# One ring of 28 rows, 12 kept rows and three spectral input buffers in a fused forward and backward pass

## The chip, the cores and the metric

The kernel runs on one core of a Trainium2 chip. The metric is the device time of one execution in microseconds (us), and lower is better. The engines are named as in the profile: PE (TensorE, matrix products), DVE (VectorE), ACT (ScalarE), POOL (GpSimd) and SP (SyncE), from whose queue every DMA of this kernel is issued. A row below is a block of 128 tokens by 512 features in bf16; there are R = 16 rows.

## The reference

With q, k, v of 2048 tokens by D = 512 features, and F = 1376 hidden features, the output is the sum of three terms:

```
xn  = layernorm(q)
kv  = (causal convolution of k with shift_k, 4 taps) * v
y   = irfft(rfft(kv padded to 4096) * rfft(ssm_k padded)) [first 2048] + kv * ssm_D
out = q + xn * y + ((xn @ w_gate) * (xn @ w_up)) @ w_down
```

Given grad_out, the kernel returns out and the gradients of q, k, v, shift_k, ssm_k, ssm_D, w_gate, w_up and w_down: ten outputs in all. The backward pass needs the same long convolution with the roles of its factors exchanged, and the products of the gated unit with respect to inputs and weights.

## The kernel before

**Stages.** The kernel is one program of about 8200 instructions with five stages that overlap.

1. *Start.* q and grad_out are loaded. DVE normalises the rows into `xn`, and PE transposes them into `XT`. A few products on constants run first.
2. *The gated unit, in six steps over F* (`glu_gen`, `mlp_rows(j, r)`). The widths of the steps are 256, 96 and four times 256 columns. For each pair of rows PE computes `pd` (grad_out by w_down) and `pg` (xn by w_gate and w_up). ACT and DVE copy them to `gu`, and DVE multiplies them into three tensors per row, called the hd rows: h, and the two factors of the gradient. They go into a ring in SBUF. `dw_gen(j)` reads 16 ring rows of a step to form the weight gradients. `hd_store(j, r)` writes them to the DRAM buffer HD. Step 5, the last one, and the last KEEP rows of step 4 are not written: `turn_gen` has PE transpose them, eight 128x128 blocks at a time, and ACT copy them back over the ring.
3. *Stage A* (`a_gen`). DVE forms the short convolution and the products kv and dy. PE applies the first factor of a Fourier transform built by hand, ACT copies the result into a buffer `ax`, and a DMA stores it to the DRAM buffer AX.
4. *The spectral stage* (`s_gen`), eight rounds i. `s_load(2i)` and `s_load(2i+1)` read AX into the buffers `sa`. `s_B(i)` applies the second factor on PE, `s_pw` multiplies the spectra on DVE, `s_Bi(i)` transforms back, and its result is stored to the DRAM buffer CX.
5. *The last stage, F,* eight chunks n of two rows. `c_load(n)` reads CX, and `last_dft(n)` applies the last factor on PE. `c_dkv`, `c_y`, `c_o5`, `c_dsk` and `dk_pair` form the gradients of v, k, ssm_k and shift_k and the term xn*y, mostly on DVE. `hd_load(n)` is a DMA transpose that reads the hd rows of two rows from HD into `hdP[n % 2]`. `y_o(n, rr)` multiplies the hd blocks by w_down for out, and `y_x(n, rr)` multiplies them by w_gate and w_up for the gradient of q. Small loads (`dkv_load`, `y_load`, `k_load`) fetch rows of v, KS (the short convolution, stored by stage A), x and k.

**What sets the order.** No queue or heuristic decides at run time. Every compute instruction and every DMA is recorded first, and `emit` replays the records in an order written out in the string `PLAN`, which also assigns each PSUM slot. The order on each engine is therefore fixed. An instruction waits when the data, the buffer or the PSUM slot is not ready, and all instructions behind it on its engine or queue wait with it. Since the recorder issues every instruction, all of them carry its line, L172, in the profile.

**Memory.** SBUF is divided by hand into regions: `rX` (xn and grad_out), the ring from 34 KB, `rT` (the transposed inputs, later the weights `wy`), `rW` (weights of the steps, later `hdP`) and `RA` (the buffers of stage A, then of the spectral stage, then of stage F, one after the other in the same bytes). The ring has 24 rows of 1536 bytes; step 0 has a 24 KB buffer of its own at `RH0`, inside `RA`. The lines that the change touches are these:

```
KEEP = 8
RING = 24
ax = [ra.tile(f"ax{i}", [128, 2, 3, D]) for i in range(2)]
ksA = ra.tile("ksA", [128, 2, D])
sp["a"] = [m.tile(f"sa{i}", [128, 2, 3, D]) for i in range(4)]
def hd_span(n):
    return (0, 1152) if 2 * n < R - KEEP else (128, 1024)
```

`hd_span` gives the rows of HD that `hd_load(n)` moves: with KEEP = 8 all 1152 rows for n = 0 to 3, and 896 for n = 4 to 7.

Of the kernel before, what the change touches and what calls it, by code (L numbers as in the profile page):

```python
# [10 lines left out]
BF = mybir.dt.bfloat16  # L11
# [17 lines left out]
KEEP = 8  # L29
RING = 24  # L30
EPS = 1e-5
PLAN = "c-k#j1GFx^4o%Xa=i0Vy+qP}nwr$(CZQHhO^L^+3Z%wCZGRf{v)~snJG#~(k0S94$AU=eH@W2oOB0?mH3<3%UQJ?^%fT$1+QbJlt1s;MR1f+(75E4Q`8i)?*pbDgi43H6GKqiO@RUr#xhOCeu3PDMT1=*ko6oyie9ZEwEhz&&{CzOHQkPGraacBW?pf2Qvvd|LBK{3b&<smLqfR0cRYCt{c1ofc=RD#Y>6RJT%XaJR=3&ew=&=qDtD`*JS;T3d)MlciFKo3X&-JvzqhMv#|5<wFf292R942NFO7HUB=NDL#OH_U?eFdjxi9q0?~U^0w?2{0SJz(i;c9bhz!fhn*W`oSa!jmcpS41lT7A6~;;m<D5EAS8qNuodRPI2Z&;U;(Uw!LSV$!CF`dOW-Xeg~hNA-oQ>+4@+SKyo2em9d^M+cn`~92<(7O@Buc%a@YeWU<<5-eee-Z!hYBdXW$fkgVV4VKEYWy4>#c}tbjvs0B*r&I1H=c9NdN5a2yVTqQiS|1X5s1yaTE5I~;`va0!mVefR;XF%70g!E|^T(&JAUjD{I7BWA)Om>GY8$AOpyvtkeq!ff~(vf~99iXkuu_Qza!5!&Ja42kXV4-CUFxCGndUtsKjtFa??!rT}N5%XYP?2HSs3wA}oZa4)e;8g66ggtN~UV+8f6MNxR=#5J;EM9}_&<B@cc+7`4AU_ts(^L>6U?D7w%drR+#bVeOS732`3gPfEti(E47oR{0jEK*mB(B1GxCSF(DSQsQa66X9gBTeXVHqro<*+<P#R^y-8(>3hgi)|DPQr&U8Fyk6jD}6|5j4Z;xE6O~b9@2oa1XY?m(UVh;XP`N>#-tM!o64-t6){!fYY!V?!)R>18ZU%+>f<zBM!&fI1)+vP<0xChj0`gz<xLyYfx3{Nn>yv)}*mmjmG0FtVMHh2F}LXG#8^|44jEos1C)%!#E%7Qg3QbNAM`d!eba4<6vKki}7$C#>W=ak2c|PT!0y=KV_oLxC1j&7D|AFDIsR1Y?PgH&{oVz11J~eraY9F@=<<Dgo$w=ZNVg%6dTbX8baG}61Akp1X7P$(RgY=^{F*Aq-5BH3Q!wrN}UL$ASK6kw3M1rXPQVkaVWK=Wi*-E(^>37!)Q32!}E9nFXAN}L6`9gUd3y89dF<ix{0^&Hr~Ozcn|O61AK^&@G(BYr}zw?V^?~CFYy(=#;NoMN77q-hwt$Ne#B4s8Bbt0nnvL%0-eTQ^aa1-H~fyL@CW|HU-%pU;9mqnB67qeq-5kNh(b_EI*FkuG=-sv6p1>}bP7u|=?oU4!W5Z`P)90CXJ{4`qvBM8N>V8*P2ngCb*HEljW*F)>Os*d2F;+D6pJ=fY>Gqc=p3D-m2{rgQ(THi7ia^mqWE-?%1~J<N9AcFRiKJAitbY-N<dpFA&sR8l!y{j5=u(R=rSdz6qJ%uQEEy<2WT`spi8uz4$>G(OX(;*t)MM*gfh@LT1|&&4OOP2w2dCpZaPeB=@IRuJ#>s7({|cL$LTlir5*H<p3n*UOMeL6J_5I&z61*LiP(K5=W4q;?lXz|MiJe2T0lQ3lKVk*-6C2@_1rH~x0vd?2F_eV*T~JLCDg_}r8#tp+PZeGy_-uN+&t>&I=RlSi+e_0-A$TL-P~=uL)~2u*V8q2x2TD0>YBOcE`+;FEnG_%(zSBETyNLfU7<cMxw}T!DVmG!Vz`*@D#dcKT^twJ#dGo94NBnNP(t^P-cll$*rjkO-Fr&qQoA%RtxM<9yAPDXWpvLelY2=oD6`Arvbt>U6(w;=U09dQy{1wwyDRO&xiYS-%i+qo@~(ob=qkC&u8OPbs=4Z}hO6mvIu`G0IVa&=kQ2$}Lb=>7f(z~XxyWvSi{e!JyFqTC8|?<WsBX9$;>Nh4E{vPvMz~>aq?_tO%P2R=g_STe!A*8!oyjye(dBVo^12|&=kmJ(uAmDc<J?>~-G!9!5>7%%Ay?SVb4A<?x70<H<!-!N<|0TES>YDDq!LwDy4fz0B$Fj>ri&(XTx2QgVn{K!$Q5_9TnQIll1oXKLKe6+uCI$JaXF>Da`W9fx7ICmu_cwPcN<)4NheVxt;ChrE|#Q`H}0)_=ia*yZljAYAKfPxPd>YZ^2L31nIw)RmTxYLB#`g!hx_UBNj%Oh@j1OD;6(DvCFDYqh%-oDNzA|9ANSW~6yU5<Knh9{E+W|^k0fQ}{1SN4c$3R6%sHi^6qXz!yvkJ;<=nE<6_s4F*;SI&?vN`kTih;JMGm`SVq99PiRU0LAt5*<hvKSIT}nzaE+wJ4wj}2=l7eeWN-is@xRxAu<>Z8`AtzmZDK8b|lxrZTT`M``&bo81p`3S(q_tddP2{3W&Fv%&UvllGv0Qdn+*NnY)seJ(-Q93)rKN=7dJ>k~NI32&;rXVEz;&gAG?$1xL|RB^iNu|xnGBW4+*P7*Q;Evac$h@zfzm}{@F0oFvACzi=3B0t43^ujhxC(Pa>vEt;d0k?mwT?i^pO#A-#u`><)Pc>21q)dE(cs+86*4MLATY-kg@W}jg!Z2n;R*!<%ydkqvWZ3=4Q!rcf@UXqh+3qm!s~5n<+coG+7|od4e2sbLFMm<8t#vnIwy3vaFLlJVnxT4qh))WtrsU-EM<q;LN;4a`AlG>sH7{$-)_Vp=^@8yjfPuQdulpWUb`m;=EOsOD5hat7MIo<Pw~XcS(LeDy4Xv?3MytnzQl_St$kixEzr(yhpZ6VJ^#uWv`Uu>U>g)@Cn&3HTjqn;sa8H_sI<@#^t#v*WyERN^Z(QY0syn19#+G(uvQ=Jvl4qq%%K|E?k)_@O`Psm*j#};oEXvD)9h*BzL4XUy+B>mG8<$>BiOgJJ;trT$LZoWvR=JxgI~22Hc&WNDsa$J-HV*<ZIG|uggbyCXM(9H|OW_NqX}O>BD`wAGhGv+@G8B7kMe4r42XZ>-<_i$agu)-{h6F<ahE@Zt!~<$fm9Mjr@?eGKjy5*TFo5f5~nBEkSyd|HvH<p||)aALG9gQit+g9>&ADEstQ-P&$%BD=FwGZpUHtvySF5JeFC<aabMCP9y4ZR-M2nSo9=E);M~KC-Nko%u_g$PUYAdMZf4Yj;hmn1}D&&9A9T~G@Z@ibPmVW@H&_0aXdZE3H1y|(6byv(`zD)uID(hX3+B-OOxn)UcgB;rY_`+dVw!;CQYV`_!58D%bZ!S@O@6MDfKF+)~uREAMykKrP(!={?NyqLVs#neZ*<>tLD&b`imEHI$gp`Ij0uWWxSkM@Ji05t2nn7)hE1~*Ki(P%O!LjKjrnjflKN}&a3&fxR%jPoL{$aDc#EDbQ^Eydt5-Db3v`3h4eLV<|0~HpYeNs!!LLTSJ9XJfp>Bx-Nmo?H<#Ak{F&dfvugU0zwkTW!)5ine&RnI(`x8m{>$ZcA79Y@e1Na&H$KRR_?jN(%6eTZY8^eoU%9Gw*BjbHn`w1zuJyEqw$z^5OM7cwt*L#qw)WM2+Fx5~Ep4s!wT(8=w%ShHYX@zp9kr8o)-Kvr2WTT5sNHmsHrBy9M4ReR9i~n6q7K(<yjs`jC0(l{be+!9+4@`O=v<wr^L2qP)J3{jm*`SmuN!ouZqjACTvzBfU8$ROi*D6zx=KgtC>^b1bgYik@j5{#>Li`4Q*^3M)9E@xx9bj_sXKL-{?XmKNB?SgyRCb5pN6shfnTx%dQcAqnxVsbN4*`<=UUU)o@$VZMX-lzc2r;JF%4(O^@N5pw3GTwPiaIutzj*NozavQ!X9Zz%V%dbiiNhwrk3BLT6Qa7i7keuvVxY?Qd=#XWiR!d*0%WeN|RY6t79KEmnE=In%fduPOEG0HIb#U51PZ?>SK*&?=+7kv9$I??`u*^XAktQUe=73-tK8(%V1YDlNGVdR@5q47K>}~EV>o5*w)?hT5*eIm93}sx29IjN?1J`U?pv!Rk4N^$4Xg68)S{Fw>7rX_FBtWA8TcAw3oHEvew4xTRCfDeQmb2wemK{+Sy!dZ#Q+Gb+B97(K_1@8*0O>lXbBMHrxtXR~u|2tb%p3>Ne79*e#o6qpX>Ywb9nXR@)j|YwK)`t+#Qu!N%K0n_ye)h#j>}cFZ>0Ry%In?1WXd?RL^8S`RyA*=(|%w&d2&&e{|^W4r8}Ewkx1)y~^Wdu?y*t-Z7P_TF~ba+_ug?1SyJ=C;Td+HTu#E$x8qv3+*XX4*$vY%}bFeX&pG{UN((OYF1Vw!L=AmRgX%W3l~ZTVZ!Cg#Te*?Vg47&n%R`VlOSU|7MTux`pwN?XNi>*8j5K#{Q3q59h=C?}29eiAC^fy!wd#s-^X-ERqL**wXp?cGJ@Pr*^|0SOy=($MG3G`nW!mkLNS{`2M*?^*MbspT%eO#e8vJ!oRTOKBh0|v-v_kfzR#>`+PpJPv}efhgQT#_H}$IZ$5{=W~F@|pWEm4NqiZf)Yta;eF0zIm-Vl#u8;0x`4m2pFX!v|7`}r4Y4v?YU&W{LZG2nb&bRj+d`Dl&ck;=6S3lGb^PPQFpVD{n!+kej&Cm2Be0N{nkMuo#P2a<h^38n%-`J1#O?*Q?&X4g;ePut(_x1z)Sl`zV^n?6(Kie1e6Z~M`$j|Y$d^4Zg&-FumAD_#&@+<u+zuK?yYyD)u&QJ9H{CdB^xA0T^M!(6Q@q7JLzuBMlOZ^Og&bRbi{0@KKZ}ao~1;5K*^z;33f5|WO`+R?Y*)Q^~{eHjQpYT`w0)N$S^^^Pof6~|R*ZgAN%OCXD{V9LLAM!W-ZhzP>@kjg{f7-9`_x%I^&_D8z{S!aUzxC7oQ~%Dt@L&8_|IL5*&-{D;!$0>s{Y(GT@9`h}EC0(M^{@SJf6V{&AN?P{%tO#8k3q}*tw3XT+gp$X-SMBj52B#E-UVsUJs%VlBFH#!keR9kx;SAI4G7bJN?@%PtOQn~8gLXK{%;U);7|>GeF6ucu(AZ=HDDyre<OeyXdMGE!4UsOzy^Us^k1|EKm&+@$E^SC{C`;ekAeh0HRa$D>?9V96__lTss(Qt92&f5Fo9s6|HA&Gq``FfpL1|nFmnrr2O<c*G<eovP5;?6a0k)}B=w&R_W8eefL*W*4)_=O-=z94{{NZ&!wlXyxJ(vYxZsNDe<}W#a&Qp?t6**cVgG3X#u7jX!~~0A<Nvkb+x`dU=BD}"
# [4 lines left out]
def kernel(  # L37
# [204 lines left out]
    rT = Region(70 * KB, 102 * KB)  # L242
    rW = Region(102 * KB, 126 * KB)
    RA = (126 * KB, 207 * KB)
    RH0 = 183 * KB
# [24 lines left out]

    def ring(j, r, n=1):
        if j == 0:
            return place([128, n, 768], BF, RH0 + 1536 * r).rearrange("p r (t f) -> p r t f", t=3)
        if j != 1:
            k = (16 * SB[j] + 16 + r) % RING
            return place([128, n, 768], BF, RH + 1536 * k).rearrange("p r (t f) -> p r t f", t=3)
        return place([128, n, 384], BF, RH + 768 * r).rearrange("p r (t f) -> p r t f", t=3)[:, :, :, 32:128]
# [7 lines left out]
    ax = [ra.tile(f"ax{i}", [128, 2, 3, D]) for i in range(2)]  # L285
# [4 lines left out]
    ksA = ra.tile("ksA", [128, 2, D])  # L290
# [31 lines left out]
    for i in range(8):  # L322
        now[0] = -40.0 + i
        MM(at0[:, 0:128], lhsT=ones1[:], rhs=ones1[:], start=True, stop=True)
    now[0] = -10.0
# [38 lines left out]
    nc.gpsimd.memset(place([128, 48, 128], BF, RH)[:, :, 0:32], 0.0)  # L364
# [54 lines left out]
    def hd_store(j, r):  # L419
        if j == 1:  # L420
            st(HP[r // 2:r // 2 + 2, 512:640].rearrange("n p e -> p n e"), place([128, 2, 768], BF, RH + 768 * r))
        else:
            e, o = hd_at(SB[j], 0), hd_at(SB[j], 1)
            st(HP[r // 2, e:o + 128].rearrange("(h p) e -> p h e", p=128)[:, ::(o - e) // 128, :], ring(j, r, 2).rearrange("p r t f -> p r (t f)"))
# [4 lines left out]
    def a_gen():  # L429
        for g in range(8):  # L430
# [3 lines left out]
            ks = ksA[:] if g < 6 else ksH[:, r0 - 12:r0 - 10, :]  # L434
# [12 lines left out]
            for rr in range(2):  # L447
                r = r0 + rr
                a = ax[r % 2]
# [14 lines left out]
    def s_alloc():  # L464
        m = Region(RA[0] + 8 * KB, RA[1])
        sp["a"] = [m.tile(f"sa{i}", [128, 2, 3, D]) for i in range(4)]
        sp["X"] = [m.tile(f"sX{i}", [128, 3, 2, D]) for i in range(3)]
        sp["Y"] = [m.tile(f"sY{i}", [128, 2, D]) for i in range(6)]
        sp["T1"] = place([128, 2, 2, D], BF, RA[0])
        sp["T2"] = m.tile("sT2", [128, 2, 2, D])  # L470
        sp["C"] = [m.tile(f"sC{i}", [128, 2, 3, D]) for i in range(2)]
        sp["E"] = [m.tile(f"sE{i}", [128, 512]) for i in range(3)]
# [10 lines left out]
    def s_load(i):  # L483
        src = AX.rearrange("(g k) r e -> (k r) g e", k=4)[:, 2 * i:2 * i + 2, :]
        ld(sp["a"][i % 4][:].rearrange("p g t d -> p g (t d)"), src)
# [546 lines left out]
```

## Time and profile before

| | |
|---|---|
| median of 5 runs | 439.15 us (437.24 to 440.83) |
| the profiled execution itself | 440.83 us |
| its span, first to last instruction | 439.0 us |
| mean granted TensorE clock | 0.998 |
| PE busy | 419.6 us (96%), 3163 products |
| DVE busy | 350.6 us (80%) |
| ACT busy | 266.6 us (61%) |
| POOL busy | 3.4 us (1%) |
| DMA queue q1, share of 16 engines | 90.7% |

The profile is one execution recorded by the hardware. Its busy rows give the time in which an engine worked; its slices cut the span in 40 equal parts and give the busy share of each in tenths; its windows give busy times in stretches that one names. A timeline lists runs of instructions with the idle time before each run and what ended it. A group row reads: line, engine, operation, output<-input, partitions x elements, count | busy us, mean ns of one | idle before. For PE the mean of one contains the pipeline, so the distance from one start to the next is the better price. What an engine waits for is read in the bracket `<-`: `<-DMA big<-HD` means that a transfer from HD into SBUF came last.

### The profile page before, as it was taken

The numbers are of one execution on the slowest core, as the hardware profiler recorded it, in microseconds if no ns is written. First come the engines' busy times: TensorE is split into PE (matmuls) and PEld (weight loads), VectorE is DVE, ScalarE is ACT, GpSimd is POOL, SyncE is SP. The second block draws the span as 40 slices with busy tenths as digits, with TensorE's granted clock in tenths as the row PEclk, the third lists the DMA queues.
The fourth block names the chain that finished last, engine by engine and source line by source line (L and its number), as shares of the span: only waits on it lengthen the run. The fifth ranks groups of instructions, "written<-read, shape, count | busy, mean of one in ns | idle before, by whom it ended". The sixth has DMA issues, their size and how long they took to land.

```text
span 439.0 us, 8183 instructions
## 1 busy us (share of the span) xinstructions
PE 419.6 (96%) x3163; PEld 201.7 (46%) x3163; DVE 350.6 (80%) x691; ACT 266.6 (61%) x367; POOL 3.4 (1%) x9
## 2 busy tenths in 40 slices
PE   5799999999999999999999999989998889999996
PEld 3366546675445443344443354445443334444443
DVE  2999877797534999899999993057396779999997
ACT  2798787665663779999989968275721303313302
POOL 1000000000000000000000010000000000000000
PEclk9999999999999999999999999999999999999999
DMA  7999879978759896889689799959999999999972
GB/s 248 407 406 349 299 272 334 381 248 283 277 209 337 262 381 202 290 273 326 206 295 296 232 298 266 312 193 328 219 261 254 274 344 265 314 322 265 278 278 74
DMA packets 94878, 124.65 MB, mean 284 GB/s; under 512 B 53748, under 2 KB 63865, under 8 KB 93816
## 3 DMA queue, kind: packets, MB, share of 16 engines
q1 hardware_dynamic: 94840, 124.13, 90.7%
q8 instruction: 25, 0.41, 0.4%
q14 instruction: 13, 0.11, 0.1%
HBM read 57.10 MB, written 54.04 MB: 253 GB/s over the span
## 4 chain that ended last, share of the span: by engine, by line
PE 60%; DVE 17%; DMA 14%; SPq 4%; ACT 2%; issue 2%; DVEq 0%; ACTq 0%
PE PP L172 60%; DVE big L172 17%; SPq L172 4%; DMA big<-HD 3%; DMA big<-CX 3%; DMA out_dram<-big 3%; ACT big L172 2%; DMA big<-in_x_dram 2%; DMA big<-in_k_dram 1%; DMA CX<-big 1%; DMA big<-in_v_dram 1%; DVEq L1028 0%; DVEq L172 0%; ACTq L172 0%
## 5 line engine op out<-in xcount | busy, mean ns | idle before, releaser
L172 PE MATMUL PP<-big 128*128 128x512 bf16 (+8 forms) x3163 | 419.6, 346 | 15.2 <-DVE big L172 4.0
L172 DVE TENSOR_TENSOR big<-big 128x1024 bf16<-128x1024 bf16 (+3 forms) x465 | 267.4, 627 | 63.3 <-ACT big L172 39.3
L172 PEld LDWEIGHTS <-big 128*128 128x128 bf16 (+5 forms) x3163 | 201.7, 97 | 232.7 <-issue 66.2
L172 ACT CAST big<-PP 128x1024 bf16<-128x1024 f32 (+2 forms) x311 | 225.3, 790 | 101.2 <-PE PP L172 70.9
L172 ACT ACTIVATE big<-big 128x512 bf16<-128x512 f32 (+3 forms) x30 | 19.0, 643 | 54.0 <-DVE big L172 53.9
L172 DVE CAST big<-PP 128x512 bf16<-128x512 f32 (+1 forms) x37 | 32.1, 871 | 12.4 <-PE PP L172 10.9
L172 ACT COPY big<-PP 128x1024 bf16<-128x1024 bf16 x25 | 25.1, 1019 | 11.5 <-PE PP L172 11.3
L172 DVE SCALAR_TENSOR_TENSOR big<-big 128x1 f32<-128x1 f32 (+2 forms) x52 | 25.0, 497 | 0.4
L172 DVE BATCH_NORM_STATS2 big<-big 128x6 f32<-128x512 bf16 x16 | 10.6, 678 | 6.7 <-DMA big<-in_x_dram 6.7
L172 DVE SCALAR_TENSOR_TENSOR big<-big,PP 128x512 f32<-128x512 bf16 x16 | 10.9, 680 | 1.2 <-PE PP L172 1.2
L172 DVE TENSOR_TENSOR big<-big,PP 128x512 bf16<-128x512 bf16 (+1 forms) x17 | 10.8, 647 | 0.0
L172 DVE TENSOR_SCALAR big<-big 128x1 f32<-128x1 f32 (+1 forms) x28 | 7.0, 258 | 0.1
L172 POOL MEMSET big<- 128x1536 bf16 (+2 forms) x3 | 2.8, 951 | 258.5 <-DVE big L172 258.5
L172 DVE BATCH_NORM_AGGREGATE big<-big 128x2 f32<-128x6 f32 x16 | 2.6, 174 | 0.0
L172 ACT ACT_TABLE_LOAD x1 | 1.3, 1283 | 0.7 <-PEq L1020 0.7
L172 DVE RECIPROCAL big<-big 128x2 f32<-128x2 f32 (+1 forms) x9 | 1.3, 154 | 0.4 <-ACT big L172 0.4
L172 DVE DVE_READ_ACCUMULATOR big<-big,PP 128x1 f32 x16 | 1.3, 81 | 0.0
L172 DVE DVE_READ_ACCUMULATOR big<-big 128x1 f32 x16 | 1.3, 81 | 0.0
L172 DVE MEMSET big<- 128x1 f32 (+1 forms) x2 | 0.2, 112 | 0.8 <-PEq L1020 0.8
L172 DVE COPY big<-PP 128x1024 bf16<-128x1024 bf16 x1 | 0.7, 672 | 0.0
masks.py:199 POOL TENSOR_SCALAR_AFFINE_SELECT big<-big 128x128 bf16<-128x128 bf16 x1 | 0.3, 296 | 0.0
masks.py:197 POOL MEMSET big<- 128x128 bf16 x1 | 0.2, 205 | 0.3 <-POOLq L1020 0.3
(4 smaller groups left out, 0.4 us busy)
## 6 DMA issues: line engine op xcount, KB each, us to landing
HD<-big SPq DMA_DIRECT2D x32, 384.0 KB, 5.4
AX<-big SPq DMA_DIRECT2D x16, 768.0 KB, 4.0
big<-AX SPq DMA_DIRECT2D x16, 768.0 KB, 6.8
CX<-big SPq DMA_DIRECT2D x32, 384.0 KB, 4.6
out_dram<-big SPq DMA_DIRECT2D x44, 256.0 KB, 3.8
big<-CX SPq DMA_DIRECT2D x7, 1536.0 KB, 7.7
big<-in_v_dram SPq DMA_DIRECT2D x16, 256.0 KB, 6.4
big<-in_w_dram SPq DMA_DIRECT2D x4, 768.0 KB, 6.8
```

Of the source, the lines that this page charges most:

```text
L172: o.fns.append(lambda: f(*[fix(x) for x in a], **{kk: fix(x) for kk, x in k.items()}))
```

## The change

The change has six parts.

- *The ring.* The ring of 24 rows and the separate buffer of step 0 become one ring of 28 rows for all six steps. `RO` gives the first row of each step. The regions behind the ring move up by 6 KB.
- *Kept rows.* KEEP goes from 8 to 12: rows 4 to 15 of step 4, not 8 to 15, stay on chip and are transposed on PE. Two `hd_store` fewer are issued, `turn_gen` transposes 24 more blocks in three more groups of eight, and `hd_load(2)` and `hd_load(3)` move 896 rows each.
- *Stage A.* There are four `ax` buffers and two `ksA` buffers.
- *The spectral stage.* There are three `sa` buffers. After `s_B(i)` the loads `s_load(2i+3)` and `s_load(2i+4)` are issued.
- *Stage F.* The x tile goes: `y_load(n)` loads x into `m[n % 2]`, two chunks ahead, once `y_x` has released it and the store from it is done. `dk` and `o5` have one buffer each.
- *Start.* Sixteen products of 128x256 on constants are recorded for the idle time at the start.

`PLAN` is a new string, so that the order and the PSUM slots of all engines differ. The counts become 3203 products (3163 before), 369 ACT instructions from the recorder (366), 272 DMAs (274), and as many on DVE and POOL.

```
-KEEP = 8
-RING = 24
+KEEP = 12
+RING = 28
+RO = [0, 16, 24, 40, 56, 72]
...
-    rT = Region(70 * KB, 102 * KB)
-    rW = Region(102 * KB, 126 * KB)
-    RA = (126 * KB, 207 * KB)
-    RH0 = 183 * KB
+    rT = Region(76 * KB, 108 * KB)
+    rW = Region(108 * KB, 132 * KB)
+    RA = (132 * KB, 207 * KB)
...
+    def slot(j, r):
+        return RH + 1536 * ((RO[j] + r) % RING)
+
     def ring(j, r, n=1):
-        if j == 0:
-            return place([128, n, 768], BF, RH0 + 1536 * r).rearrange("p r (t f) -> p r t f", t=3)
         if j != 1:
-            k = (16 * SB[j] + 16 + r) % RING
-            return place([128, n, 768], BF, RH + 1536 * k).rearrange("p r (t f) -> p r t f", t=3)
+            return place([128, n, 768], BF, slot(j, r)).rearrange("p r (t f) -> p r t f", t=3)
...
-    ax = [ra.tile(f"ax{i}", [128, 2, 3, D]) for i in range(2)]
+    ax = [ra.tile(f"ax{i}", [128, 2, 3, D]) for i in range(4)]
-    ksA = ra.tile("ksA", [128, 2, D])
+    ksA = [ra.tile(f"ksA{i}", [128, 2, D]) for i in range(2)]
...
+    for i in range(16):
+        now[0] = 2 + 0.5 * i
+        MM(at0[:, 0:256], lhsT=ones1[:], rhs=ones1[:].unsqueeze(1).to_broadcast((128, 2, 128)), start=True, stop=True)
...
-        sp["a"] = [m.tile(f"sa{i}", [128, 2, 3, D]) for i in range(4)]
+        sp["a"] = [m.tile(f"sa{i}", [128, 2, 3, D]) for i in range(3)]
...
-        ld(sp["a"][i % 4][:].rearrange("p g t d -> p g (t d)"), src)
+        ld(sp["a"][i % 3][:].rearrange("p g t d -> p g (t d)"), src)
...
-            if i < 6:
-                s_load(2 * i + 4)
-                s_load(2 * i + 5)
+            for k in (2 * i + 3, 2 * i + 4):
+                if k < 16:
+                    s_load(k)
...
-                ACOPY(place([128, 8, 128], BF, RH + 1536 * ((16 * SB[j] + 16 + r0) % RING) + 256 * k), pt)
+                r, b = blk[k][0], k % 6
+                ACOPY(place([128, 8, 128], BF, slot(j, r) + 256 * b), pt)
...
-        f["x"] = m.tile("fx", [128, 2, D])
-        for n in ("m", "e", "dk"):
+        f["dk"] = m.tile("fdk", [128, 2, D])
+        f["o5"] = m.tile("fo5", [128, 2, D])
+        for n in ("m", "e"):
             f[n] = [m.tile(f"f{n}{i}", [128, 2, D]) for i in range(2)]
-        f["o5"] = [m.tile(f"fo5{i}", [128, 2, D]) for i in range(2)]
...
     def y_load(n):
-        ld(f["x"][:], x_d[:, 2 * n:2 * n + 2, :])
+        ld(f["m"][n % 2][:], x_d[:, 2 * n:2 * n + 2, :])
...
-        TT(m[:], xn[:, rs, :], f["y"][:], op=ALU.mult)
-        TT(m[:], f["x"][:], m[:], op=ALU.add)
+        TT(f["tmp"][:], xn[:, rs, :], f["y"][:], op=ALU.mult)
+        TT(m[:], m[:], f["tmp"][:], op=ALU.add)
         TT(e[:], go[:, rs, :], f["y"][:], op=ALU.mult)
-        if n + 1 < NCH:
-            y_load(n + 1)
...
             y_x(n, 1)
             if n + 2 < NCH:
+                y_load(n + 2)
                 hd_load(n + 2)
```

## The prediction

> **What bounds the kernel now.** I read the busy row first, then the slices, then the windows of each stage, and last the PE's idle gaps.
>
> ```profile
> PE 419.6 (96%) x3163; PEld 201.7 (46%) x3163; DVE 350.6 (80%) x691; ACT 266.6 (61%) x367; POOL 3.4 (1%) x9
> PE   5799999999999999999999999989998889999996
> DVE  2999877797534999899999993057396779999997
> PEclk9999999999999999999999999999999999999999
> ```
>
> TensorE (PE) is busy in 96% of the span at the full granted clock. Only the two ends and slices 27 to 32 fall below nine tenths. The windows by stage put numbers on that (columns: window and length; then PE, PEld, DVE, ACT, POOL busy; PE clock; DMA share; GB/s):
>
> ```profile
> 130.00:240.00 110.00, 109.83 (x1069) 47.64 (x1068) 99.60 (x180) 92.79 (x120) 0.00 (x0) 1.00 0.84 285
> 285.00:375.00 90.00, 83.43 (x515) 38.76 (x514) 66.06 (x134) 35.28 (x39) 0.00 (x0) 1.00 1.04 268
> 375.00:439.00 64.00, 59.01 (x317) 26.67 (x313) 60.90 (x132) 15.88 (x18) 0.00 (x0) 0.99 0.91 254
> ```
>
> From 30 to 285 us PE has no gap worth naming. Here one more product costs its own time, and one more VectorE (DVE) or ScalarE (ACT) operation costs nothing until a product waits for it. From 285 to 375 us PE loses 6.6 us while the DMA engines are full. From 375 us DVE is at 95% (60.9 of 64) as well. PE's timeline at 326 to 348 us shows what it waits for (start, length, what, and in brackets the idle time before and who ended it):
>
> ```profile
> 325.79 7.08 PE L172 MATMUL PP<-big 128*128 128x512 bf16 x38
> 334.60 11.09 PE L172 MATMUL PP<-big 128*128 128x512 bf16 x56 [1.72 <-DMA big<-HD]
> 347.12 1.25 PE L172 MATMUL PP<-big 128*128 128x512 bf16 x5 [1.44 <-DMA big<-HD]
> ```
>
> These are hd_load(2) and hd_load(3). SP's queue, which issues every DMA, stands still during each of them:
>
> ```profile
> 301.34 12.73 SPq L172 DMA_TRANSPOSE big<-HD  x1
> 319.67 11.54 SPq L172 DMA_TRANSPOSE big<-HD  x1
> 335.90 9.18 SPq L172 DMA_TRANSPOSE big<-HD  x1
> ```
>
> The other gaps after 285 us are 1.84 us at 285.2 (the first last_dft waits for the last quarter of c_load(0)), 1.19 at 356.1 (DVE waits for k_load(3), issued behind hd_load(3)), 0.71 at 414.2, and 0.19 and 0.15 at 316 and 322. Without the 0.71 this is about 6.5 us; other short pauses bring it to 6.95. At the end the last product is done at 434.75 us, DVE at 435.98, and the last store lands at 437.79.
>
> **What the Trainium skill says.** "TensorE: Matmul & The Clock Gate", section "Wait — 56ns, not 53.3ns?": back-to-back products start N/2.4 GHz plus about 2.5 ns apart when warm and N/1.2 GHz apart when cold. The trace agrees: 56, 109 and 216 ns for 128, 256 and 512 columns, and 427 ns for the first eight products. Its section "What's actually happening" lets the clock fall after an idle window of about 3.4 us. The start's only long gap, 2.88 us at 6.0, is shorter, and the 256-column products after it start 109 ns apart, so they are warm. "Perfetto Trace Analysis", "Identifying the Most-Contended Engine", warns that matmul occupancy is no measure of the distance from the peak; I therefore use start-to-start times, not the mean of 381 ns in the group row. "DMA: Bandwidth & Descriptors", "Issuing engines are not separate DMA queues": all transfers share 16 engines. Here SP issues all of them, so a held queue delays every later one.
>
> **The change, part by part.** I laid the new order of every engine's instructions, read from the two programs, against the old one and took durations from the rows of before.
>
> *Products and copies.* Rows 4 to 7 of step 4 are now transposed on PE: 4 rows x 3 tensors x 2 blocks = 24 products at 0.056 = +1.35 us, in a stretch where PE is full, so all of it on the path. Three more ACT copies at 1.02 us (group row, 25.1/25) lie where ACT is 72% busy (32.2 of 45): hidden; uncovered they would cost 3.06. The 16 idle-time products (16 x 0.109 = 1.75 us) lie in the start's idle time, before x lands at 10.80 us. The products after the gap are already warm, so they gain nothing; 0 taken, 0 to +0.5. Two stores to HD fewer free SP for about a microsecond in a stretch where PE doesn't wait for it: 0. The x tile and the second dk and o5 tiles go, with no instruction less.
>
> *The tail.* After the last last_dft DVE still has 25.5 us of work in the new order and PE 21.4, so DVE has 4.1 us more; before it was 26.4 and 24.6, or 1.8 more (the 0.71 us that PE waited at 414.2 and the 1.23 from its last product to DVE's end). Products moved out of this stretch run earlier, at the same cost. Near the end: after the last y_x block PE has 3.2 us of products left (before 5.6), while 6.7 us of DVE work stands queued. So the end comes about 2.3 us later against PE, with 0.1 for the store's start: **+2.4**. Bounds are 0 (PE late for another reason, so that DVE catches up) and +3.5 (the whole 6.7 less 3.2).
>
> *The hd waits.* hd_load(2) and (3) move 896 of 1152 rows. On before's rows a full one held SP for 9.2 to 12.7 us and landed after 14.3 to 14.9; a reduced one held it 8.1 to 10.1 and landed after 11.8 to 12.3. With the new order each of hd_load(2) to (7) has 2 to 4 us to spare. So 1.72 and 1.44 go, and the 1.19 that came from SP held in hd_load(3): **-4.35**. What is late next:
> - *c_load(0).* Its last quarter still stands behind hd_load(0) on SP, and PE reaches the first last_dft about 19 us after the last s_Bi. I take 2.4 us (1.7 to 3.5) against 1.84: +0.55; the second last_dft 0.4.
> - *hd_load(1).* From the last weight-gradient product to the first use of hdP[1] PE has 18.7 us of work instead of 22.3 (where it waited 0.19). The transpose waits for a store to leave and follows y_o(0)'s store on SP. Short of 3.6 us: I take 2.2 (1 to 3.7), +2.0.
> - *k, x, v and KS loads in the middle of stage F.* y_load(4), (5) and k_load(5) now stand behind transposes, and y_load waits for the store of the row pair before (it reuses m). DVE waits, and behind it the additions that free PSUM: 1.0 (0 to 4), as 1.19 was paid for one such load.
>
> Before's 6.95 thus becomes 2.4 + 0.4 + 2.2 + 1.0 = 6.0, plus the next item.
>
> *Three spectral inputs, not four.* After s_B(i) only s_load(2i+3) must land before s_B(i+1). Between the first rounds PE has 5.2, 5.6, 8.7 and 6.7 us of work, later 11 to 12. The first of a pair landed after 4.3 to 7.1 us in before: **+0.7** (0 to 5.3). Taken together with the hd waits: 6.7 - 6.95 = -0.25.
>
> *Stage A.* More ax and ksA buffers can only take waits away; PE shows none from 30 to 130 us (busy 100.00 of 100): 0. At the start the transposes' copy now precedes the pd copy on ACT, and part of the 1.24 us gap at 15.9 goes: -0.3 (-1 to +0.5).
>
> Sum: 1.35 + 2.4 - 0.25 - 0.3 = **+3.2 us**. The profiled execution took 440.83 us (span 439.0), so it would become 444.0. The median of the runs shown is 439.15, 1.7 lower, and there I expect **442.4**.
>
> **Rivals.**
> - *The waits go and none takes their place (faster).* For: both transposes shrink and each has slack; before waited only 0.19 for hd_load(1). Only 1.0 us of waits remain: 1.35 + 2.4 - 6.95 + 1.0 - 0.3 = -2.5, so 436.6. It decides where hd_load(1) lands less than 12 us after its issue and c_load(0)'s quarter before PE comes. Against: no transpose of before landed sooner than 11.8.
> - *The spectral stage starves (slower).* If each input takes the 7.1 us of the slow ones plus 0.5 for the issue, rounds 0 to 3 lose (7.6 - 5.2) + (7.6 - 5.6) + (7.6 - 6.7) = 5.3 instead of 0.7: +7.8, so 447. For: no more slack than that. Against: several inputs landed after 4.3.
> - *Waits only change place (no change).* The tail's DVE work turns out to fit beside PE, which is late anyway: 3.2 - 2.4 = +0.8, so 440.
> - *The change doesn't do what it says.* If the new order left hd_load(2) and (3) just as late, -3.2 would fall away: 445.6. The smaller transfers speak against it.
>
> **How the numbers follow.** About 0.5% (2.2 us) is what a measurement of this kernel can tell from no change: the limits are 436.95 and 441.35. The forecast of 442.4 gets 0.48, of which a tenth lies under 441.35; the first rival 0.19; the second and the fourth together 0.16; the third 0.17. So faster 0.19, same 0.05 + 0.17 = 0.22, slower 0.59. The likeliest case alone spans 440 to 445.5. The range holding 8 in 10 runs from 436.5, where the waits go, to 448, where the spectral stage starves.
>
> **What would show it.** Right: in the trace after, no wait for big<-HD at hd_load(2) and (3); one of 1 to 4 us at hd_load(1); a gap of about 2.4 before the first last_dft; DVE at work some 4.6 us after the last product; 240 products of 128x128 and 28 copies of 128x1024. Wrong: PE gaps in the spectral stretch (130 to 275 us) over 2 us in all, or gaps after 285 us adding up to less than 2 us, or DVE ending within 2 us of PE.

## The result, and the profile after

The changed kernel takes 436.81 us in the median of 43 runs (434.72 to 439.1), and the kernel before beside it 438.8 us (80 runs). The ratio is 0.9971, with a 95% interval of 0.9956 to 0.9985: faster by 0.3%. All ratios here compare fast runs alone (none over 1.5% above the fastest of its kernel), so they are not the quotients of the medians, and the profiled execution of the kernel before, 440.83 us, is not among the fast ones. Run again on another occasion (the run after_again), the change gave 436.07 us and a ratio of 0.9924 (0.9895 to 0.9953). A small gain is shown both times; the two intervals do not overlap, so its size stays open between 0.15 and 1.05%. I had forecast 442.4 us, slower by 0.7%. The first rival, in which the waits go and none takes their place, had said 436.6.

The busy row, the slices of PE and DVE and the clock of the profile after:

```profile
PE 420.7 (97%) x3203; PEld 204.2 (47%) x3203; DVE 352.9 (81%) x691; ACT 266.9 (61%) x370; POOL 3.5 (1%) x9
PE   7799999999999999999999999989999999999993
DVE  2989999968548999899999871057657999899996
PEclk9999999999999999999999999999999999999997
```

The dip of PE in slices 31 to 33 is gone; slice 27 still shows 8 tenths, and the last slice falls to 3. The windows (columns as before):

```profile
130.00:240.00 110.00, 110.00 (x1099) 47.25 (x1096) 104.27 (x189) 95.17 (x122) 0.00 (x0) 1.00 0.73 246
285.00:375.00 90.00, 89.23 (x536) 41.52 (x535) 72.48 (x148) 35.89 (x41) 0.00 (x0) 1.00 1.04 286
375.00:436.00 61.00, 53.00 (x281) 23.93 (x279) 55.22 (x118) 12.64 (x15) 0.00 (x0) 0.95 0.78 227
```

From 130 to 240 us PE works without a pause although the spectral stage has three input buffers. From 285 to 375 us it loses 0.77 us, not 6.6, with the DMA engines as full as before. PE's timeline from 282 us shows what is left:

```profile
282.71 1.49 PE L173 MATMUL PP<-big 128*64 128x512 bf16 x12 [0.30 <-DMA big<-CX]
284.75 8.41 PE L173 MATMUL PP<-big 128*128 128x512 bf16 x56 [0.56 <-ACT big L173]
293.93 126.29 PE L173 MATMUL PP<-big 128*64 128x512 bf16 x716 [0.77 <-DMA big<-CX]
```

The first last_dft waits 0.30 us, then products of the last weight gradient fill the time, and the second last_dft waits 0.77. From then on PE works nearly without a pause. No wait of PE for big<-HD is left, at hd_load(1) either. SP's timeline shows why (start, length of the hold; the first line is c_load(2)):

```profile
295.45 0.57 SPq L173 DMA_DIRECT2D big<-CX  x1
...
305.90 7.84 SPq L173 DMA_TRANSPOSE big<-HD  x1
...
317.38 8.31 SPq L173 DMA_TRANSPOSE big<-HD  x1
...
331.63 6.68 SPq L173 DMA_TRANSPOSE big<-HD  x1
```

hd_load(1), a full transpose, holds SP for 7.84 us, where it held it for 12.73 before. The other two hold it for 8.31 and 6.68 us instead of 11.54 and 9.18.

The bill of the two profiled executions: PE's waits after its first product fall from 14.10 to 6.45 us in all (before 30 us from 6.61 to 4.60, after it from 7.49 to 1.85). PE is busy 1.1 us longer, although the 40 added products were priced at 3.1; what became of the other 2 us is not shown. The last product ends 6.5 us earlier, at 428.22 instead of 434.76. DVE ends 4.42 us after it instead of 1.22, so 3.2 us are given back. The spans differ by 3.4 us (439.0 and 435.6). The last products of the kernel before, and below them the last products of the changed kernel and the last DVE instructions (start, length):

```profile
414.93 19.83 PE L172 MATMUL PP<-big 128*128 128x512 bf16 x107 [0.71 <-ACT big L172]
```

```profile
374.75 53.47 PE L173 MATMUL PP<-big 128*128 128x512 bf16 x281
...
431.02 1.62 DVE L173 TENSOR_TENSOR big<-big 128x1024 bf16<-128x1024 bf16 x3
```

### The profile page after: what moved, and what is told of

Same layout as the page of the kernel before. It is cut to its first block, busy times and chain, and to the rows that moved or that the text cites. A ratio compares the mean times of both kernels' runs of the same rounds, so it can differ in the third digit from the quotient of the medians.

```text
span 435.6 us, 8231 instructions
## 1 busy us (share of the span) xinstructions
PE 420.7 (97%) x3203; PEld 204.2 (47%) x3203; DVE 352.9 (81%) x691; ACT 266.9 (61%) x370; POOL 3.5 (1%) x9
## 4 chain that ended last, share of the span: by engine, by line
PE 86%; DMA 9%; SPq 1%; DVE 1%; ACT 1%; issue 0%; DVEq 0%; ACTq 0%
PE PP L173 86%; DMA big<-HD 4%; DMA big<-CX 3%; DMA big<-in_x_dram 2%; SPq L173 1%; DVE big L173 1%; ACT big L173 1%; DMA out_dram<-big 0%; DVEq L1032 0%; DVEq L173 0%; ACTq L173 0%
## 5 line engine op out<-in xcount | busy, mean ns | idle before, releaser
L173 PE MATMUL PP<-big 128*128 128x512 bf16 (+9 forms) x3203 | 420.7, 345 | 7.5 <-DVE big L173 2.9
L173 PEld LDWEIGHTS <-big 128*128 128x128 bf16 (+5 forms) x3203 | 204.2, 97 | 223.5 <-issue 65.2
L173 DVE TENSOR_TENSOR big<-big 128x1024 bf16<-128x1024 bf16 (+4 forms) x465 | 267.5, 629 | 44.0 <-ACT big L173 39.3
L173 ACT CAST big<-PP 128x512 bf16<-128x512 f32 (+2 forms) x311 | 223.3, 785 | 75.1 <-PE PP L173 61.4
L173 ACT COPY big<-PP 128x1024 bf16<-128x1024 bf16 x28 | 27.8, 1025 | 5.1 <-PE PP L173 5.1
```

The source lines that it names most:

```text
L173: o.fns.append(lambda: f(*[fix(x) for x in a], **{kk: fix(x) for kk, x in k.items()}))
```

## The experiments

The medians of the kernel before beside these runs were 438.47 (first group), 437.90 (second) and 439.42 (third). Ratios are formed as above. The groups ran on three different chips, so kernels of different groups are better compared by their ratios than by their times.

### What the kept rows and the size of the transfers do

**keep8.** One constant of the changed kernel goes back, and `PLAN` with it: the three groups of transposes leave it, and the two stores to HD return.

```
-KEEP = 12
+KEEP = 8
```

> The changed kernel with KEEP back at 8 and everything else as changed (28 ring rows, its order with the three groups of transposes taken out and two stores to HD put back; hd_load(2) and (3) move 1152 rows again). Theory A, the kept rows bring the gain (smaller transposes free SP and land in time): PE waits of 1 us or more at hd_load(2) or (3) come back, and the time is 438.5 to 440.5 us, as before. Theory B, the new order brings it and the kept rows cost their 24 products: no such wait, and the time is 435.0 to 436.5, some 0.7 to 1.3 us below the changed kernel's 436.8.

Measured: 443.54 us, ratio 1.0105 (1.0055 to 1.0154). Theory A holds in its direction and is too small. The new order without the kept rows is 1% slower than the old kernel. The waits are not at the hd_loads, however, but at two last_dfts that wait for CX. PE's timeline of keep8:

```profile
282.72 67.97 PE L173 MATMUL PP<-big 128*64 128x512 bf16 x417 [2.24 <-DMA big<-CX]
354.70 7.55 PE L173 MATMUL PP<-big 128*64 128x512 bf16 x32 [4.00 <-DMA big<-CX]
```

The second wait is last_dft(4): c_load(4) is late behind the full transposes. The first line shows a second thing. Without the 24 products PE reached the first last_dft earlier, and started it at 282.72 us, where the changed kernel starts it at 282.71. The load that it waits for sets this point, and the 24 products were done in that wait.

**full23.** The changed kernel with only the size of two transfers put back:

```
-        return (0, 1152) if 2 * n < R - KEEP else (128, 1024)
+        return (0, 1152) if n < 4 else (128, 1024)
...
-        ldT(..., in_=HP[n, a:b])
+        ldT(..., in_=HP[n - 2 if 2 <= n < 4 else n, a:b])
```

> The changed kernel with hd_load(2) and (3) at 1152 rows (they read chunks 0 and 1 of HD, so that the products of row pairs 2 and 3 take other rows' numbers) and the 24 transposes kept: the size of the two transfers alone. Theory A (size): SP is held 1 to 3 us longer in each, PE waits at them, +1 to +3 us, so 438 to 440. Theory B (order): each has 2 to 4 us to spare, the time stays within 0.7 us of 436.8.

Measured: 439.07 us, ratio 1.0038 (1.0013 to 1.0063). That is 2.3 us above the changed kernel, so theory A in the time. hd_load(2) held SP for 10.59 us and hd_load(3) for 9.62. The slack that I had counted for each was eaten, and the wait came out at last_dft(4), 2.62 us, not at the hd_loads.

keep8 beside it, in the same group, is 4.5 us slower still. It moves as many rows in these two loads, lacks the 24 products and has two stores to HD more. The windows behind the first last_dft, of keep8 and below it of full23, show one part of this (the third figure from the end is PE's granted clock):

```profile
284.00:288.00 4.00, 3.85 (x14) 1.35 (x11) 1.90 (x3) 3.82 (x5) 0.00 (x0) 0.60 1.01 351
```

```profile
284.00:288.00 4.00, 3.42 (x19) 1.56 (x16) 1.76 (x3) 3.81 (x5) 0.00 (x0) 1.00 1.06 397
```

In keep8 PE waited 2.24 us there and then worked at half the clock; with the products the wait was 0.57 us, and the clock stayed up. So the products, priced at +1.35, cost nothing in this place, and in this execution their absence did.

**small23.** The other way round: the kernel before with only those two transfers reduced.

```
-        return (0, 1152) if 2 * n < R - KEEP else (128, 1024)
+        return (0, 1152) if n < 2 else (128, 1024)
```

> The kernel before with hd_load(2) and (3) at 896 rows (the products of blocks 6 and 7 of rows 4 to 7 take other blocks' numbers), nothing else: the smaller transfers in the old order. Theory A (size): the 1.72 and 1.44 us waits at hd_load(2) and (3) and the 1.19 us behind them shrink by 2 us or more in all, so 436 to 437. Theory B (order): hd_load(1), held 12.7 us, still makes everything behind it late; less than 1 us gained, 438 to 439.

Measured: 436.63 us, ratio 0.9972 (0.9948 to 0.9997), the same as the whole change beside its own runs (0.9971), and 1.8 us below the median of the kernel before: theory A, with an interval that just excludes 1. After the first last_dft PE does not wait again:

```profile
287.71 142.93 PE L172 MATMUL PP<-big 128*64 128x512 bf16 x827 [2.03 <-DMA big<-CX]
```

The 1.72, 1.44, 1.19 and 0.71 us waits are all gone. That the size of the two transfers took them away is shown by the times, not by this profile alone: with full transfers in the old order idle_before waited 1.47 and 1.74 us for big<-HD, but before_again, below, not at all.

### What holds a transpose

**cload_ahead.** One DMA of the changed kernel is moved in `PLAN`: c_load(2), the 12th before hd_load(1), goes directly ahead of it.

> The changed kernel with c_load(2) issued directly ahead of hd_load(1), not 13 DMAs earlier, as the kernel before had it. Theory A (a DMA transpose's hold on SP contains what is still moving ahead of it): SP is held 11 to 13 us in hd_load(1) instead of 7.8, though it moves the same 1152 rows, and hd_load(2) comes 3 to 5 us later. Theory B (the hold is the transpose's own work): 7.5 to 9 us, and only last_dft(2) is late.

Measured: 445.45 us (one run). SP's timeline of cload_ahead:

```profile
304.92 0.60 SPq L173 DMA_DIRECT2D big<-CX  x1
305.58 12.07 SPq L173 DMA_TRANSPOSE big<-HD  x1
```

Theory A: the same transpose holds SP for 12.07 us with 1.5 MB ahead of it, and for 7.84 us when c_load(2) landed at 302.74, before it was issued. hd_load(2) was issued 8.5 us later than in the changed kernel, more than theory A's 3 to 5, and last_dft(2) waited 6.10 us. It is one pair of profiles, but the nine profiles of the new order with c_load(2) early all lie between 7.84 and 9.09 us. In the kernel before, c_load(2) was issued 1.8 us ahead of hd_load(1) and landed at 308.65, 7.3 us after hd_load(1) was issued. That fits its 12.73 us, but does not fully explain them. In before_again the distance is the same, c_load(2) landed 5.3 us after the issue, and the hold was shorter:

```profile
302.36 0.62 SPq L172 DMA_DIRECT2D big<-CX  x1
304.19 9.33 SPq L172 DMA_TRANSPOSE big<-HD  x1
```

The four profiles in the old order held SP in hd_load(1) for 9.05 (small23), 9.33, 12.02 (idle_before) and 12.73 us. What decides between them is open.

### What the idle-time products do

**noidle and noidle_again.** The changed kernel without them, twice:

```
-    for i in range(16):
-        now[0] = 2 + 0.5 * i
-        MM(at0[:, 0:256], ...)
```

> The changed kernel without the 16 idle-time products. They took about 2.1 us of PE in the start, whose waits are 4.6 us instead of 6.6. Theory A (they lie in idle time, the clock was up already): PE's waits in the first 30 us rise back by about 2 us, all later work begins at the same time, within 0.5 us of 436.8. Theory B (they push the first steps back): 0.5 to 1.5 us faster. Theory C (they keep the clock up): the first 128x512 products after the wait for the transposed gradient start over 300 ns apart and the time grows by 0.5 us or more.

Measured: 440.12 us, ratio 1.0021 (0.9997 to 1.0045), 3.3 us above the changed kernel: the time of theory C without its sign. In the profile (438.97 us, 1.6 above the profiled execution of the changed kernel) the clock stayed up and the work from 20 us on began 0.6 us earlier, but PE waited 4.05 us after 240 us, where it waits 1.85 in the changed kernel. Whether such waits belong to the kernel, one execution can't tell. Hence a second run of it beside a second run of the changed kernel.

> The changed kernel without the 16 idle-time products, a second time. Theory A (without them the clock falls in the start in part of the executions; the first profile missed it): again 439 to 441 us, mean granted clock of the runs near 0.992, and in this profile a stretch at half rate in the first 20 us or after a wait in the last stage. Theory B (the first result was the chip's): within 1 us of the changed kernel beside it.

> The changed kernel as it is, a second time beside the next two. If the ranking of the variants belongs to the kernels, it comes out at 436 to 437.5 again; if it belongs to the chip or the hour, it moves with the others by more than 1 us. Its second profile shows which of the waits of the last stage stay the same from one execution to the next.

Measured: 439.46 us without the products (14 runs, ratio 0.9998, 0.9968 to 1.0028) and 436.07 us with them (11 runs). The difference of 3.4 us is the one of the first time, so it belongs to the kernels. This time the profile shows a fall of the clock. The windows of noidle_again, and below them those of the changed kernel (PE's granted clock is again the third figure from the end):

```profile
8.00:12.00 4.00, 1.81 (x16) 1.46 (x16) 1.40 (x4) 0.78 (x2) 0.00 (x0) 0.78 1.01 387
12.00:16.00 4.00, 3.48 (x9) 1.04 (x9) 3.36 (x12) 0.78 (x2) 0.00 (x0) 0.50 1.03 396
```

```profile
8.00:12.00 4.00, 2.75 (x28) 2.28 (x29) 1.50 (x5) 0.59 (x1) 0.00 (x0) 1.00 1.01 368
12.00:16.00 4.00, 3.01 (x21) 1.59 (x22) 4.00 (x12) 2.59 (x6) 0.00 (x0) 1.00 1.05 415
```

Without the products the clock was at half from 10.3 to 17.1 us, and PE reached the steady part at 22.68 us, against 20.41 and 20.79 in the two profiles of the changed kernel. The mean clock of each run tells how often: it is at or below 0.992 in 20 of the 36 runs without the products and in none of the 55 with them. Theory A holds for the clock. That the clock makes up all of the 3.4 us was not shown: those 20 runs have a median of 440.58 us, and the other 16 still one of 439.13, over 2 us above the changed kernel. (The mean is a rough sign, since it also takes in the end of the span, where the clock falls in every profile once PE has finished.)

**idle_before.** The same 16 products put into the kernel before, ahead of and behind the products of rows 2 and 3 and behind the first transposes.

> The kernel before with the 16 idle-time products put into its start (four before the products of rows 2 and 3, five before and seven after the first transposes) and nothing else. Theory A: they keep the clock up. In the run with the small transfers in the old order, which has no such products, the 512-column products after the 2.44 us wait at 9 us started 427 ns apart for 3.4 us. Such a fall then happens in part of the executions, and with the products the time falls by 0.8 to 2 us, to 436.6 to 437.8, and the mean granted clock of the runs rises above the 0.995 of before. Theory B (the start's waits hide everything): within 0.5 us of 438.5 and the same clock. Theory C (they stand in front of real products): 0.5 to 1.5 us slower.

Measured: 441.50 us, ratio 1.007 (1.0038 to 1.0102). Theory A failed for this order, and the loss is larger than theory C's. PE still waited 1.98 us behind the products, and the clock was at half from 13.1 to 16.5 us in the profile:

```profile
12.29 4.90 PE L172 MATMUL PP<-big 128*128 128x512 bf16 x23 [1.98 <-DVE big L172]
```

The work behind the start began about 1.2 us later than in before's first profile, and the first last_dft waited 2.72 us. Where such products stand matters; why seven of them, up to 10.3 us, were not enough is open.

**before_again.** The kernel before as it is, for a second profile.

> The kernel before as it is, for a second profile. If the waits of the last stage belong to the kernel, 1 us or more at hd_load(2) and (3) and at the first last_dft come again; if the clock falls in part of its executions, a stretch at half rate in the first 20 us or after a wait of 2 us may be seen, which the first profile (mean clock 0.998) did not have. Either way 436 to 441 us.

Measured: 438.69 us (one run). No hd_load was waited for: their holds were 9.33, 9.98 and 7.62 us instead of 12.73, 11.54 and 9.18. Instead the clock fell, in the start and after the wait of 2.25 us before the first last_dft:

```profile
8.00:12.00 4.00, 2.31 (x17) 1.80 (x18) 1.62 (x5) 0.58 (x1) 0.00 (x0) 0.66 1.04 389
12.00:16.00 4.00, 4.00 (x12) 1.61 (x13) 2.65 (x9) 1.25 (x3) 0.00 (x0) 0.50 1.04 409
284.00:292.00 8.00, 5.42 (x27) 2.45 (x27) 1.27 (x2) 3.33 (x5) 0.00 (x0) 0.82 0.32 113
```

So the same kernel lost time in different places in two executions that differ by 2 us in their spans. The old kernel's times are spread accordingly: the standard deviation is 2.2 us over its 80 runs, and 1.2 over the 43 of the changed kernel.

### What the end costs

**tail_none.** The changed kernel without seven DVE instructions at the end:

```
-        for j in range(4):
+        for j in range(4 if r0 < 14 else 0):
```

> The changed kernel without the seven DVE instructions of the last dk_pair (the last two rows of the gradient of k keep old data). They take 4.2 us on DVE's queue at the end. Theory A (DVE's queue sets the end, which comes 4.4 us after the last product): 2 to 3.2 us less, 433.6 to 434.8. Theory B (the last chain through y_o and y_x sets the end): less than 0.8 us gained.

Measured: 435.59 us, ratio 0.9948 (0.9925 to 0.9971). That is 1.2 us less than 436.81, between the theories, but the two ratios of the changed kernel, 0.9971 and 0.9924, lie on both sides of it, so no gain is shown. In the profile DVE ended 2.98 us after the last product instead of 4.42. It did 4.2 us less work, but waited 2.23 us for something else (its timeline):

```profile
428.12 0.75 DVE L173 SCALAR_TENSOR_TENSOR big<-big 128x512 f32<-128x512 bf16 x1 [2.23 <-DMA out_dram<-big]
```

The same wait is 0.55 us in the changed kernel:

```profile
429.15 0.75 DVE L173 SCALAR_TENSOR_TENSOR big<-big 128x512 f32<-128x512 bf16 x1 [0.55 <-DMA out_dram<-big]
```

The store issued last before it is psd_end's, of the gradient of shift_k (at 427.32 us in the changed kernel).

**tail_pool.** The last dk_pair on POOL:

```
+        if r0 == R - 2:
+            acc = f["ks"]; tmp = f["v"]; T = nc.gpsimd.tensor_tensor
...
-            TT(dst[:], dks_rows(r0 + j), skb(f["sk"], j, 2), op=ALU.mult)
+            T(dst[:], dks_rows(r0 + j), skb(f["sk"], j, 2), op=ALU.mult)
...
-                TT(acc[:], acc[:], tmp[:], op=ALU.add)
+                T(acc[:], acc[:], tmp[:], op=ALU.add)
```

> The changed kernel with the last dk_pair on POOL, into buffers that are free by then (the tiles of v and ks). Theory A (DVE's queue sets the end): if POOL needs less than about 2.5 us for one of the seven, 1.5 to 3 us less than the changed kernel, 433.8 to 435.3. Theory B (POOL is slow or holds DVE up): POOL ends last, or DVE's instructions in the last 20 us grow beyond 0.75 us each, and the time is 437 or more.

Measured: 448.98 us, ratio 1.023 (1.0188 to 1.0272). Theory B. The group of POOL, and DVE's timeline beside it:

```profile
L173 POOL TENSOR_TENSOR big<-big 128x1024 bf16<-128x1024 bf16 x7 | 17.5, 2511 | 144.1 <-DVE big L173 143.7
```

```profile
413.66 2.61 DVE L173 TENSOR_TENSOR big<-big 128x1024 bf16<-128x1024 bf16 x1
...
421.32 2.59 DVE L173 TENSOR_TENSOR big<-big 128x1024 bf16<-128x1024 bf16 x1
```

POOL needs 2.51 us for one, which is about the limit that I had set. But DVE's additions and products of the same size, 0.68 us each in the changed kernel, take 2.0 to 2.61 us meanwhile. PE waits 6.2 and 3.3 us for DVE, and works at half the clock from 422.3 to 435.9 us.

**tail_act.** The last four rows' sum on PE and ACT, and psd_end's store last:

```
...
+                MM(po[:, c], lhsT=ident[:], rhs=m[:, rr, c], start=False, stop=True)
+                ACOPY(m[:, rr, c], po[:, c])
```

> The changed kernel with the last four rows' sum in y_o made by one more product by the identity (4 x 0.216 us) and copied out by ACT, in place of five DVE additions (3 x 0.68 + 2 x 0.41 us), and with psd_end's store issued last. Theory A (DVE's queue sets the end, and a DVE wait of 0.55 us for that store's landing at 429.1 goes): DVE ends about 2 to 3 us earlier and PE 0.9 us later, 434.0 to 435.5 us. Theory B (the copies make PSUM or ACT late, or the chain after y_x's last product sets the end): 436 or more.

Measured: 436.11 us (6 runs), ratio 0.9909 (0.9874 to 0.9945), beside 436.07 us for the changed kernel in the same group. The time is theory B's, though theory A's mechanism is there: in the profile DVE no longer waits for the store, and it ends 2.97 us after the last product instead of 4.42. Of these 1.45 us the five products by the identity, three of 512 columns and two of 256, take 0.9 back at the price of 0.216 us for 512, and no gain is left that these runs can tell.

## Why the prediction was wrong, point by point

The forecast was +3.2 us, and the two profiled executions differ by -3.4. In the terms of its sum:

- The waits after 30 us, without the 0.71, are 6.78 us in the trace before (the 6.95 is 0.2 too high). They were to fall by 0.25 and fell by 4.9, to 1.85.
- The tail was to cost 2.4 and cost 2.5, the 3.2 us above less the 0.71 that the prediction counts in this term.
- PE's own work, idle-time products apart, was to grow by 1.35. It shrank by 0.65 (1.1 less their 1.75), for a reason that is not shown.
- The start was to gain 0.3 and did: its waits fell by 2.0, and the idle-time products fill 1.75 of that.

So the step that failed is "What is late next": it put 6.0 us of waits into the last stage, and 1.85 came. This is 4.7 of the 6.6 us by which the forecast missed the profile. The prediction had named this sign of being wrong, gaps after 285 us of less than 2 us in all (0.99 here). A second step failed that the two profiles do not show, the 0 for the idle-time products. Point by point:

- *What bounds the kernel:* right for PE, incomplete for the rest. One execution was read as the kernel. Its clock did not fall before PE had finished, and before_again's fell twice; its waits for big<-HD were not there in before_again.
- *24 products, +1.35 us on the path:* wrong. They were hidden before the first last_dft, which starts at 282.7 us with them and without them (keep8).
- *16 idle-time products, 0:* wrong by the medians: taking them out of the new order costs 3.3 and 3.4 us. The step is "The products after the gap are already warm, so they gain nothing". It was true of the one execution shown. That the clock falls more often without them is shown (20 of 36 runs against none of 55); that this makes up the whole amount is not.
- *The hd waits, -4.35:* right for the profiled execution. small23 and full23 show that the size of the two transfers matters, but on the median it is worth less: 1.8 us in the old order and 2.3 in the new one.
- *What is late next, +2.0 for hd_load(1):* wrong, 0 measured. I priced a full transpose at 9.2 to 12.7 us of SP, the holds of before's trace, without asking what moved ahead of each. The new order issues c_load(2) early enough, the hold is 7.84, and the 3.6 us that PE comes sooner are made up. cload_ahead brings 12.07 back.
- *2.4 and 0.4 us at the first two last_dfts:* too high as a sum, 1.07 instead of 2.8 (0.30 and 0.77). The last quarter of c_load(0) does stand behind hd_load(0) in the new order: SP was held until 277.88 us, and the load was issued at 278.67. But it landed 4.0 us later, at 282.67, when PE had just come. In the order before it was issued at 281.15, once the last store to CX had landed at 281.0; the last four of these stores had left SP only after hd_load(0), from 273.86 us on. The new order puts the stores ahead of hd_load(0), and the last of them landed at 272.86. That I had not counted.
- *Loads in the middle of stage F, +1.0:* too high; the waits after 295 us are 0.22 us in the profile.
- *Three spectral inputs, +0.7:* 0 measured. The second rival, starvation, is excluded: 110.00 of 110 us busy.
- *The tail, +2.4:* right, as above. DVE ends 4.42 us after the last product (4.6 forecast). But it is not DVE's work alone: tail_none takes 4.2 us of it away, and DVE ends only 1.4 us sooner behind the last product, since it then waits for a store.
- *The start, -0.3:* right in these two profiles, as above.

The first rival, with 1.0 us of waits left, came nearest, and its condition was named in the prediction: hd_load(1) landing in less than 12 us. The profile after does not record this landing; tail_act's, in the same order, has 11.10 us. That its 436.6 meets 436.81 so well is partly luck: it charged 1.35 us for products that were hidden, and nothing in it stands for what the idle-time products are worth. What the new order alone contributes was not isolated. With full transposes it is slower than the old one, without the idle-time products it is no faster than the old one, and small23 in the old order reaches the same time as the whole change.

## What to carry to other kernels

A DMA's length in a trace is its price in that place and in that execution. Before a held queue is used as a price, look at what was issued ahead of it and when that landed. And one profiled execution shows one way to lose time: compare its clock with the clocks of the other runs before a clock effect or a wait is booked at zero or in full.

## What the runs showed of the hardware

- A DMA transpose of 1152 rows held SP for 7.84 us when the load of 1.5 MB ahead of it had landed, and for 12.07 us directly behind that load. The same transpose in the same order held it for 12.73 us in one execution and 9.33 in another.
- In the last stage every single wait of PE of 2.03 us or more was followed by products at half the clock: 2.03 us (small23), 2.24 (keep8), 2.25 (before_again) and 2.72 (idle_before) at the first last_dft, 2.62 and 4.00 at last_dft(4) (full23, keep8), 6.10 at last_dft(2) (cload_ahead), 6.21 near the end (tail_pool). No wait of 1.84 us (before) or less was. Most of these waits are shorter than the idle window of about 3.4 us in the Trainium skill ("TensorE: Matmul & The Clock Gate", "What's actually happening"), which I had leaned on; the measurement decides. In the start there was no such limit: 1.98 us (full23), 2.79 (after_again) and 2.88 (before) passed without a fall, while 1.98 (idle_before), 2.03 (before_again), 2.13 (noidle_again) and 2.44 (small23) brought one.
- In the clock records of the traces these falls last 3.41 us each, or a multiple (6.83 in before_again's start, noidle_again and cload_ahead, 13.65 in tail_pool). By estimate from this, one of 3.41 us at half the clock costs a full PE 1.7 us.
- POOL's 128x1024 bf16 additions and products took 2.51 us each, and DVE's own instructions of that size beside them grew from 0.68 to as much as 2.61 us.
